# v_m times the input weights in pairs of blocks, on half rows and quarter columns of TensorE

## The chip, the cores and the metric

The kernel runs on one core of one Trainium2 chip. A core has a matrix engine (TensorE, in the profile PE, with its weight loads as PEld), which multiplies a stationary operand of up to 128 rows by 128 columns by a moving operand and writes to banks of PSUM; three elementwise engines, VectorE (DVE), ScalarE (ACT) and GpSimd (POOL); and DMA queues, here issued from SyncE (SP). Each engine works through its own instructions in order and waits on semaphores for the others. The metric is the device time of one execution in microseconds. The kernel before took 1661.22 us (median of 3 runs, 1661.06 to 1661.4).

## The reference

For 8 batches of 8 heads, 576 tokens, head size 64 and 32 memory slots, the reference compresses keys and values to 32 slots a head, attends to them, and puts the 4608 tokens through two pairs of dense layers:

```
a = softmax(phi) over the 32 slots
k_m = einsum('bhsm,bhsd->bhmd', a, k);  v_m = einsum('bhsm,bhsd->bhmd', a, v)
attn = softmax(q @ k_m.T / 8) over the slots
x = (attn @ v_m) as 4608 tokens x 512 (head h has columns 64h to 64h+63)
h = x @ w_in (512 x 2048);  g = max(0.01*h, h);  x = g @ w_out
out = (sigmoid(x @ w_gate) * (x @ w_val)) @ w2_out
```

What matters here is that `attn @ v_m @ w_in` is computed as `attn @ (v_m @ w_in)`: for each batch the product of v_m (32 slots of 8 heads, so 256 rows) and w_in is made once, and the tokens' attention is multiplied by that.

## The kernel before

**Two halves.** Until about 837 us the kernel does attention and the first pair of layers, batch by batch; after that the gated pair, which the change does not touch.

**Units and parts.** The attention of a batch is two units `(b, g)` of four heads each: unit 0 has heads 0 to 3, unit 1 heads 4 to 7. A unit is cut into parts: `t1`, `t2`, `t7a`, `t7b`, `t4`, `t5`, `t8a`, `t8b` are TensorE work, and `v1` to `v11` the work of the other engines between them. `t4` makes k_m and v_m of the four heads in one PSUM bank (`ps_kv`), 16 matmuls of 128 rows by 32 columns and 4 of 64 rows, each head on its own quarter of the columns. `v5` scales them by the softmax sums: two ACT copies (L520) write k_m and v_m with a mask, so that each head's 64 columns stand in the left or right half and zeros in the other. `t5` transposes that (`ps_kvT`), `v6` copies it to `kvT`. `t8a`, `t8b` make the scores (`ps_sc`), which `v8a`, `v8b` transpose out of PSUM on DVE (L577).

**v_m times w_in.** `vw_block(b, j)` (L646 to L660) makes 256 columns of the product, block j of 8, for both units: four matmuls (L651) of all 128 rows by 64 columns, with 256 moving columns each, into one PSUM bank `ps_vw` of 512 columns. Half of each stationary operand's entries are the zeros of the mask. The operands are plain fp32, for which the trace shows two matmul records and two weight loads to one instruction. Its `done()` evacuates the bank with `split`: an ACT copy to a rounded high part (L160) and a DVE subtraction for the low part (L161), both 128x512.

**Steps.** The first pair of layers is 256 steps, 32 a batch: a step is one half of the batch's tokens (288) by 128 of the 2048 middle columns. `m1_in` (L678) multiplies the attention (`at_hi`, `at_lo`) by 128 columns of the batch's `vw` into `ps_h`, 6 matmuls; an ACT activation reads `ps_h` (L683, `gr`); `split` makes `gh` on ACT and `gl` mostly on POOL; `m1_out` (L700) multiplies these by `w_out` into four accumulators, 12 matmuls. The main loop at step i issues: the split of step i+1; `m1_in` of step i+2; the `v` parts of units and the conversion jobs of that step, round robin (`run(vs)`), at their head the `done()` of a block from the step before (`held`); the `t` parts; a `vw_block`, if one is due; and last `m1_out` of step i. So a block's bank is read out one step after it is made.

**What sets the order.** Numbers in `SCHED`: `chain` and `chain1` give the step of each part from the unit's start, `unit` and `units` the starts, and `vw`, `vw1`, `vw2` the steps at which the 8 blocks of a batch are made (counted from the start of the batch before; `vw1` and `vw2` from the first step). Blocks of batch 0 are made by `first_vw` while weights are still being converted. The `t` parts and the blocks share two PSUM banks (`psa`, pool `ps_a`), taken in turn: each new user waits until the one two before has been read out. The `vw` tiles have nine buffers.

Of the kernel before, what the change touches and what calls it, by code (L numbers as in the profile page):

```python
# [8 lines left out]
F32 = mybir.dt.float32  # L9
# [47 lines left out]
           'v11': 16},  # L57
 'units': [1, 13, 30, 42],
 'unit': [-8, 8],
# [3 lines left out]
 'groups': [4, 4, 4, 2, 1, 1],  # L63
 'chain1': {'lp': -9,
            'lk': -4,
# [28 lines left out]
def tile_kernel(  # L94
# [42 lines left out]
    gp = ctx.enter_context(tc.tile_pool(name="g", bufs=3))  # L137
    p1 = ExitStack()
    cvp = p1.enter_context(tc.tile_pool(name="cvp", bufs=2))
    dr = ctx.enter_context(tc.tile_pool(name="dr", bufs=1, space=bass.MemoryType.DRAM))  # L140
    ps_acc = ctx.enter_context(tc.tile_pool(name="ps_acc", bufs=4, space=bass.MemoryType.PSUM))
    ps_h = ctx.enter_context(tc.tile_pool(name="ps_h", bufs=2, space=bass.MemoryType.PSUM))
# [5 lines left out]

    ident = const.tile([P, P], F32, name="ident")
    ones = const.tile([P, P], F32, name="ones")  # L150
    mask = const.tile([P, 2], F32, name="mask")

    def f32(ap):
        return ap.bitcast(F32)
# [208 lines left out]

    def unit_phi(u):
        b, g = u
        hs = slice(HG * g, HG * g + HG)
        s = un.setdefault(u, {})
        s["ph"] = ap_.tile([P, HG, CC, M], F32, tag="ph", name="ph")
        if u == FIRST2:
            m = s["m0"] = wtile("vw", [P, 2 * PC], F32, "unit_a")  # L370
            s["pht"] = m[:ST, 896:1024].rearrange("p (h m) -> p h m", h=HG)
        else:
            s["pht"] = ap_.tile([ST, HG, M], F32, tag="pht", name="pht")
        nc.sync.dma_start(
            out=s["ph"].rearrange("p h c m -> p h (c m)"),
            in_=phi[b, hs, 0:SM, :].rearrange("h (p c) m -> p h (c m)", c=CC),
        )
        nc.sync.dma_start(out=s["pht"], in_=phi[b, hs, SM:S, :].rearrange("h p m -> p h m"))

    def unit_kv(u):  # L380
        b, g = u
        hs = slice(HG * g, HG * g + HG)
        s = un[u]
        if u == FIRST2:
            m1_ = cvp.tile([P, 2 * PC], F32, tag="raw", name="unit_b", bufs=2)
            m2_ = s["m2"] = cvp.tile([P, 2 * PC], F32, tag="raw", name="unit_c", bufs=2)
            flat = (pbuf.rearrange("p c f -> p (c f)")[:, 0:1024], m1_)
            s["kv"] = [t.rearrange("p (i h c d) -> p i h c d", i=2, h=2, c=CC) for t in flat]
            s["kvt"] = m2_[:ST, 0:512].rearrange("p (i h d) -> p i h d", i=2, h=HG)
        else:  # L390
            t = ap_.tile([P, 2, HG, CC, D], F32, tag="kv", name="kv")
            s["kv"] = [t[:, :, 2 * j:2 * j + 2] for j in range(2)]
            s["kvt"] = ap_.tile([ST, 2, HG, D], F32, tag="kvt", name="kvt")
        for i, src in enumerate((k, v)):
            for j in range(2) if u == FIRST2 else (None,):
                dst = t[:, i] if j is None else s["kv"][j][:, i]
                hj = hs if j is None else slice(hs.start + 2 * j, hs.start + 2 * j + 2)
                nc.sync.dma_start(
                    out=dst.rearrange("p h c d -> p h (c d)"),
                    in_=src[b, hj, 0:SM, :].rearrange("h (p c) d -> p h (c d)", c=CC),  # L400
                )
            nc.sync.dma_start(out=s["kvt"][:, i], in_=src[b, hs, SM:S, :].rearrange("h p d -> p h d"))

    def unit_q(u):
        b, g = u
        hs = slice(HG * g, HG * g + HG)
        s = un[u]
        if u == FIRST2:
            s["q"] = obuf.rearrange("p c f -> p (c f)")[:, 0:1024].rearrange("p (c h d) -> p c h d", c=CC, h=HG)
            s["qt"] = s["m2"][:ST, 512:768].rearrange("p (h d) -> p h d", h=HG)  # L410
        else:
            s["q"] = ap_.tile([P, CC, HG, D], F32, tag="q", name="q")
            s["qt"] = ap_.tile([ST, HG, D], F32, tag="qt", name="qt")
        for c in range(CC):
            nc.sync.dma_start(
                out=s["q"][:, c], in_=q[b, hs, 0:SM, :].rearrange("h (p c) d -> c p h d", c=CC)[c],
            )
        nc.sync.dma_start(out=s["qt"], in_=q[b, hs, SM:S, :].rearrange("h p d -> p h d"))
# [4 lines left out]
    def psa(name):  # L423
        return ps_a.tile([P, 512], F32, tag="a", name=name)
# [82 lines left out]
    def v5(u):  # L507
        s = un[u]
        p = s.pop("p")
        r = ap_.tile([P, 2], F32, tag="r", name="r", bufs=2)  # L510
        nc.vector.tensor_scalar_add(r[:, 0:1], p[:, 4 * D:4 * D + 1], 1e-9)
        yield
        nc.vector.reciprocal(r[:, 0:1], r[:, 0:1])
        yield
        nc.vector.tensor_scalar_mul(r, mask, r[:, 0:1])
        yield
        x = etile(u)
        x = s["x"] = x.rearrange("p a m -> p (a m)")[:, 0:4 * D].rearrange("p (a f) -> p a f", a=2)
        for j in range(2):
            nc.scalar.activation(  # L520
                x[:, :, j * D:(j + 1) * D], p[:, 0:2 * D].rearrange("p (a d) -> p a d", a=2), AF.Copy, scale=r[:, j:j + 1]
            )
        yield

# [118 lines left out]
        for i in range(2):  # L643
            PARTS[n + "ab"[i]] = lambda u, f=f, i=i: f(u, i)

    def vw_block(b, j):  # L646
        p = psa("ps_vw")
        for g in range(NG):
            t = kvT[b, g]
            for i in range(2):  # L650
                nc.tensor.matmul(  # L651
                    p[64 * i:64 * i + 64, g * VB:(g + 1) * VB],
                    t[:, 1, 64 * i:64 * i + 64], win[j][:, 2 * g + i, :], start=True, stop=True,
                )
        def done():
            t = vw[b, j] = wtile("vw", [P, 2, NG, VB], F32R, "vw")
            split(p.rearrange("p (g f) -> p g f", g=NG), t[:, 0], t[:, 1])
            yield

        return done  # L660

    hps = {}
    gt = {}
# [286 lines left out]
    with tc.manual_schedule():  # L950
        make_identity(nc, ident)
        nc.vector.memset(ones, 1.0)
        nc.vector.memset(mask, 0.0)
        for h in range(HG):
            nc.vector.memset(mask[32 * h:32 * h + 32, h % 2:h % 2 + 1], 1.0)

# [66 lines left out]
        VW_AT = {b: [(b - 1) * NS + x for x in SCHED["vw"]] for b in range(3, B)}  # L1023
        VW_AT[0] = {i: n + NVB - len(SCHED["vw0"]) for n, i in enumerate(SCHED["vw0"])}
        VW_AT[1], VW_AT[2] = SCHED["vw1"], SCHED["vw2"]

# [8 lines left out]

        def first_vw(j):
            done_until(4 * j + 2)
            return vw_block(0, j)

        def unit_parts(i):  # L1040
            vs, ts_, ls = [], [], []
# [68 lines left out]
        for i, (b, hf, fc) in enumerate(steps):  # L1110
            if fin:
                fin()
                fin = None
            if i + LA < len(steps):
                fin = step_in(*steps[i + LA])
            else:
                if not tmps:
                    tmp_open()
                next(first)
                next(first)  # L1120
            vs, ts_, ls = unit_parts(i)
# [12 lines left out]
            run(vs)  # L1134
            for f, u in ts_:
                f(u)
            if i in VW_AT[0]:
                held = first_vw(VW_AT[0][i])
            for n in {b, b + 1} - {0}:
                if i in VW_AT.get(n, []):  # L1140
                    held = vw_block(n, VW_AT[n].index(i))
            m1_out(b, hf, fc)
            for f, u in ls:
                f(u)
            if b == B - 1:
# [69 lines left out]
```

## Time and profile before

| | before |
|---|---|
| median of 3 runs | 1661.22 us |
| the profiled execution, its whole time | 1660.55 us |
| its span, first to last instruction | 1658.8 us |
| PE busy | 1606.2 us, 97% of the span |
| DVE, ACT, POOL busy | 853.0, 681.1, 434.6 us |
| PE busy with `ps_vw` (L651) | 71.4 us, 512 records |

The page gives the busy time of each engine, a strip of the span in 40 slices, the chain of work that ended last, and the costliest groups of instructions. The profiled execution is 1.75 us longer than its span, and 0.67 us shorter than the median. Matmuls are pipelined: each record's duration holds its way through the array, so records overlap, and what a group of matmuls costs is read from start to start.

### The profile page before, as it was taken

The page shows a single profiled execution, that of the slowest core. Times are in us where ns is not written, and L with a number is a line of the kernel's source. Part 1 is how long each engine was busy: PE and PEld are TensorE (multiplying, and loading weights), DVE is VectorE, ACT ScalarE, POOL GpSimd, SP SyncE. Part 2 cuts the span into 40 slices and gives each one's busy share as a digit, 9 for nine tenths or more (in the row PEclk, how much of TensorE's full clock was granted, in tenths as well). Part 3 has the DMA queues.
Part 4 walks back from the last instruction along what each step waited for, and adds up shares of the span by engine and source line. Part 5 has one row for each costly group of instructions (what it writes and reads, how often), then busy time and mean ns, then how long its engine had stood idle before and what let it go on. Part 6 is the DMA issues. An engine that isn't in the chain of part 4 may idle for free.

```text
span 1658.8 us, 26089 instructions
## 1 busy us (share of the span) xinstructions
PE 1606.2 (97%) x9976; PEld 1390.8 (84%) x9976; DVE 853.0 (51%) x1467; ACT 681.1 (41%) x1516; POOL 434.6 (26%) x429
## 2 busy tenths in 40 slices
PE   4688999999999999999999999999999999999998
PEld 2577898989899898989988888888888888888897
DVE  6998555454454455532133655454653465354544
ACT  4664455555455555544532223331333142222332
POOL 2777343454434444443300002000200011000100
PEclk8799999999999999999999999999999999999999
DMA  9712353454445354412455466564475456546692
GB/s 297 264 45 76 105 167 102 138 158 148 135 135 168 109 156 130 148 65 78 142 154 191 139 200 192 167 219 146 144 257 176 142 170 219 167 137 201 210 401 77
DMA packets 169021, 268.58 MB, mean 162 GB/s; under 512 B 60608, under 2 KB 105664, under 8 KB 168896
## 3 DMA queue, kind: packets, MB, share of 16 engines
q1 hardware_dynamic: 168896, 266.91, 51.1%
q8 instruction: 79, 1.29, 0.3%
q14 instruction: 46, 0.38, 0.1%
HBM read 219.68 MB, written 47.19 MB: 161 GB/s over the span
## 4 chain that ended last, share of the span: by engine, by line
PE 58%; DMA 0%; DVE 0%; ACT 0%; issue 0%; SPq 0%; ACTq 0%
PE oacc L906 18%; PE ps_y L808 13%; PE ps_z L808 9%; PE ps_x L808 9%; PE acc L700 6%; PE ps_h L678 3%; PE ps_vw L651 0%; DMA gvs<-hl 0%; PE ps_kv L502 0%; PE ps_sc L567 0%; DVE hl L298 0%; PE ps_qT L550 0%; DVE st L603 0%; ACT e L596 0%; DVE osum L917 0%
## 5 line engine op out<-in xcount | busy, mean ns | idle before, releaser
L700 PE MATMUL acc<-gh,wo 128*128 128x288 f32 x2048 | 433.7, 304 | 0.6 <-ACT gh L160 0.6
L700 PEld LDWEIGHTS acc<-gh,wo 128*128 128x128 f32 x2048 | 326.3, 189 | 37.8 <-ACT gr L683 19.5
L161 POOL TENSOR_TENSOR gl<-gr,gh 128x288 fp32r<-128x288 f32 x250 | 221.5, 889 | 333.4 <-ACT gh L160 206.2
L700 PE MATMUL acc<-gl,wo 128*128 128x288 f32 x1024 | 303.7, 297 | 1.9 <-POOL gl L161 1.9
L906 PE MATMUL oacc<-w2t,pt 128*128 128x512 f32 x1296 | 296.3, 389 | 0.0
L906 PEld LDWEIGHTS oacc<-w2t,pt 128*128 128x128 f32 x1296 | 243.1, 188 | 50.3
L808 PE MATMUL ps_y<-xo,wt 128*128 128x512 f32 (+1 forms) x1080 | 251.9, 369 | 0.0
L683 ACT ACTIVATE gr<-ps_h 128x288 f32<-128x288 f32 x256 | 105.6, 413 | 325.7 <-PE ps_h L678 294.6
L678 PE MATMUL ps_h<-at_hi,vw 128*128 128x288 f32 x1024 | 213.6, 297 | 8.5 <-ACT vw L160 6.6
L808 PEld LDWEIGHTS ps_y<-xo,wt 128*128 128x128 f32 x1080 | 190.4, 188 | 33.9
L771 POOL TENSOR_TENSOR xo<-xr,xo 128x512 fp32r<-128x512 f32 (+1 forms) x16 | 23.0, 1460 | 671.0 <-ACT xo L767 671.0
L700 PEld LDWEIGHTS acc<-gl,wo 128*128 128x128 f32 x1024 | 193.3, 189 | 2.8 <-POOL gl L161 2.6
L678 PEld LDWEIGHTS ps_h<-at_hi,vw 128*128 128x128 f32 x1024 | 166.1, 190 | 9.6 <-ACT vw L160 7.5
L808 PE MATMUL ps_z<-xo,wt 128*128 128x512 f32 (+1 forms) x720 | 167.4, 368 | 0.3 <-ACT pt L843 0.3
L808 PE MATMUL ps_x<-xo,wt 128*128 128x512 f32 (+1 forms) x720 | 167.5, 368 | 0.0
L678 PE MATMUL ps_h<-at_lo,vw 128*128 128x288 f32 x512 | 151.4, 296 | 0.0
L808 PEld LDWEIGHTS ps_x<-xo,wt 128*128 128x128 f32 x720 | 127.2, 188 | 22.9
L808 PEld LDWEIGHTS ps_z<-xo,wt 128*128 128x128 f32 x720 | 127.1, 189 | 23.0 <-ACT pt L843 0.5
L843 ACT CAST pt<-sg 128x512 fp32r<-128x512 f32 (+1 forms) x120 | 69.6, 580 | 182.1 <-DVE sg L836 182.1
L161 DVE TENSOR_TENSOR vw<-ps_vw,vw 128x512 fp32r<-128x512 f32 x64 | 44.1, 691 | 183.1 <-ACT vw L160 183.1
L160 ACT CAST gh<-gr 128x288 fp32r<-128x288 f32 x256 | 112.0, 437 | 1.6
L678 PEld LDWEIGHTS ps_h<-at_lo,vw 128*128 128x128 f32 x512 | 97.1, 190 | 0.0
(155 smaller groups left out, 1804.3 us busy)
## 6 DMA issues: line engine op xcount, KB each, us to landing
wt<-gvs SPq DMA_DIRECT2D x210, 512.0 KB, 4.5
w2t<-w2s SPq DMA_DIRECT2D x60, 512.0 KB, 5.8
gvs<-hl SPq DMA_DIRECT2D x84, 256.0 KB, 2.3
x2s<-obuf SPq DMA_DIRECT2D x15, 576.0 KB, 3.5
win<-in_moe_w_in_dram SPq DMA_DIRECT2D x16, 512.0 KB, 8.9
wo_bits<-in_moe_w_out_dram SPq DMA_DIRECT2D x16, 512.0 KB, 9.0
xr<-x2s SPq DMA_DIRECT2D x16, 512.0 KB, 6.5
q<-in_q_dram SPq DMA_DIRECT2D x60, 128.0 KB, 5.1
```

The lines of the kernel that those rows point to most:

```text
L160: nc.scalar.copy(hi, raw)
L161: eng.tensor_sub(lo, raw, f32(hi))
L678: nc.tensor.matmul(p[:, :HALF], w, x, start=(n == 0), stop=(n == 3 * NG - 1))
L683: nc.scalar.activation(gr, p[:, :HALF], AF.Prelu, alpha=0.01)
L700: nc.tensor.matmul(a[d][:, :HALF], w[:, ds_], x, start=(open_ and n == 0), stop=(close and n == 2),)
L771: eng.tensor_sub(t[:, 1, :h], x_operand(n, k, a), f32(t[:, 0, :h]))
L808: nc.tensor.matmul(bank, w[:, l, a, :], x[:, r, :h], start=(start and i == 0), stop=(i == 5), skip_group_check=not start,)
L843: nc.scalar.copy(d[:, 0, :h], s)
L906: nc.tensor.matmul(bank[i], pt[2 * f + t][:, l, q * P:(q + 1) * P], w2t[f][:, r, :], start=(f == 0 and l + r == 0), stop=(f == TH - 1 and ...
```

## The change

- Unit g now has every second head (g, g+2, g+4, g+6): the four inputs are viewed as `b (h g) s d`. Shapes, sizes and number of the loads stay.
- `v5` writes k_m as before, but v_m otherwise. For batches 1 to 7 it puts each head's v_m in both halves (one ACT copy of 128x128 that reads its source twice); k_m takes two copies of 128x64. For batch 0 v_m goes into half g alone, zeros into the other, with two more mask columns; that is four copies of 128x64.
- Batch 0: `vw_block(j)` makes a block with eight matmuls of 128 rows by 32 columns instead of four of 64 columns; evacuation as before.
- Batches 1 to 7: `vw_pair(b, j0)` makes two blocks at once, with 16 matmuls of 64 rows (half g of the array, where unit g's copy lies) by 32 columns (a head's quarter). Unit g writes to its own bank; so a pair takes both banks of `ps_a`. In program order the halves alternate, then the quarters, then the block.
- The pair's evacuation is issued in the same step, behind the step's other work: four ACT copies and four DVE subtractions of 128x256. `held` is left to batch 0.
- Four pairs a batch instead of eight blocks, at other steps: 20, 22, 36, 38 (the last batch 20, 22, 25, 28; batch 1 at 26, 28, 31, 37; batch 2 at 54, 57, 59, 63).

```diff
- 'vw': [20, 21, 22, 23, 25, 27, 31, 33],
- 'vw1': [25, 27, 28, 29, 31, 33, 37, 39],
- 'vw2': [54, 55, 57, 59, 64, 68, 71, 73],
+ 'vw': [20, 22, 36, 38],
+ 'vw_last': [20, 22, 25, 28],
+ 'vw1': [26, 28, 31, 37],
+ 'vw2': [54, 57, 59, 63],
...
+    q, k, v, phi = (x.rearrange("b (h g) s d -> b g h s d", g=NG) for x in (q, k, v, phi))
...
         for j in range(2):
+            nc.scalar.activation(x[:, 0, j * D:(j + 1) * D], p[:, 0:D], AF.Copy, scale=r[:, j:j + 1])
+        if u[0] == 0:
+            for j in range(2):
+                m = 2 if j == u[1] else 3
+                nc.scalar.activation(x[:, 1, j * D:(j + 1) * D], p[:, D:2 * D], AF.Copy, scale=r[:, m:m + 1])
+        else:
             nc.scalar.activation(
-                x[:, :, j * D:(j + 1) * D], p[:, 0:2 * D].rearrange("p (a d) -> p a d", a=2), AF.Copy, scale=r[:, j:j + 1]
+                x[:, 1, :].rearrange("p (a d) -> p a d", a=2),
+                p[:, D:2 * D].rearrange("p (a d) -> p a d", a=1).to_broadcast([P, 2, D]), AF.Copy, scale=r[:, 2:3],
             )
...
+    def vw_pair(b, j0):
+        js = (j0, j0 + 1)
+        ps = [psa("ps_vw") for _ in range(NG)]
+        for n, j in enumerate(js):
+            for h in range(HG):
+                for g in range(NG):
+                    nc.tensor.matmul(
+                        ps[g][M * h:M * h + M, n * VB:(n + 1) * VB],
+                        kvT[b, g][D * g:D * g + D, 1, M * h:M * h + M],
+                        win[j][D * g:D * g + D, h, :], start=True, stop=True,
+                    )
+        for j in js:
+            vw[b, j] = wtile("vw", [P, 2, NG, VB], F32R, "vw")
+        for g in range(NG):
+            for n, j in enumerate(js):
+                split(ps[g][:, n * VB:(n + 1) * VB], vw[b, j][:, 0, g], vw[b, j][:, 1, g])
...
-                    held = vw_block(n, VW_AT[n].index(i))
+                    vw_pair(n, 2 * VW_AT[n].index(i))
```

On PE, at step 20 of batch 5 (where batch 6's first product is made), the program has before, from `m1_in` to the next block:

```order
L678 MATMUL ps_h<-at_hi,vw 128x288 x2
L678 MATMUL ps_h<-at_lo,vw 128x288
L651 MATMUL ps_vw<-win,kvT 64x256 x4
L700 MATMUL acc<-gh,wo 128x288 x2
L700 MATMUL acc<-gl,wo 128x288
```

and now, at the same step:

```order
L705 MATMUL ps_h<-at_hi,vw 128x288 x2
L705 MATMUL ps_h<-at_lo,vw 128x288
L678 MATMUL ps_vw<-win,kvT 32x256 x16
L727 MATMUL acc<-gh,wo 128x288 x2
L727 MATMUL acc<-gl,wo 128x288
```

The product stands at the same place between `m1_in` of step i+2 and `m1_out` of step i; four instructions became sixteen of half the output rows, and the block that stood in the next step is gone.

On ACT, at step 37 (part `v5` of batch 2's first unit, `e<-ps_kv,r`), before:

```order
L160 CAST gh<-gr 128x288
L683 ACTIVATE gr<-ps_h 128x288
L520 ACTIVATE e<-ps_kv,r 128x2x64 x2
L160 CAST gh<-gr 128x288
L683 ACTIVATE gr<-ps_h 128x288
L160 CAST vw<-ps_vw 128x512
L160 CAST gh<-gr 128x288
```

and now:

```order
L162 CAST gh<-gr 128x288
L710 ACTIVATE gr<-ps_h 128x288
L521 ACTIVATE e<-ps_kv,r 128x64 x2
L527 ACTIVATE e<-ps_kv,r 128x128
L162 CAST vw<-ps_vw 128x256 x4
L162 CAST gh<-gr 128x288
L710 ACTIVATE gr<-ps_h 128x288
```

The block's copy stood behind the next step's `gh` and `gr`; the pair's four copies stand in the pair's own step, ahead of the next step's `gh`, and directly behind the copies out of `ps_kv`, whose bank the pair takes.

## Rows read from the trace of the kernel before

**Rows 1.** The page: busy time (share of the span) and instructions.

```profile
PE 1606.2 (97%) x9976; PEld 1390.8 (84%) x9976; DVE 853.0 (51%) x1467; ACT 681.1 (41%) x1516; POOL 434.6 (26%) x429
```

**Rows 2.** Busy time by stretch, all engines; columns as in the first line.

```profile
core 0: us, PE busy (x) PEld busy (x) DVE busy (x) ACT busy (x) POOL busy (x), PEclk, DMA share, GB/s
...
560.00:660.00 100.00, 100.00 (x797) 90.42 (x796) 48.63 (x97) 53.20 (x138) 43.72 (x46) 1.00 0.47 136
```

**Rows 3.** Who waited for whom on PE, 160 to 840 us: total, times, longest.

```profile
PE acc L700 <- POOL gl L161: 0.4, 1, 0.4
PE acc L700 <- ACT gh L160: 0.2, 1, 0.2
```

**Rows 4.** Groups by line and shape: busy us, mean ns of one.

```profile
L651 PE MATMUL ps_vw<-win,kvT 128*64 128x256 f32 x512 | 71.4, 400 | 5.9 <-POOL win L210 4.1 <-issue 1.7
...
L541 ACT COPY kvT<-ps_kvT 128x256 f32<-128x256 f32 x16 | 5.9, 369 | 1.2 <-PE ps_kvT L531 1.2
...
L879 DVE TENSOR_TENSOR sg<-ps_y,tmp 128x256 f32<-128x256 f32 x6 | 2.5, 425 | 6.5 <-PE ps_y L808 6.5
```

**Rows 5.** PE in order of time, a step with a block, 664 to 669 us.

```profile
664.83 0.43 PE L678 MATMUL ps_h<-at_hi,vw 128*128 128x288 f32 x2
...
665.49 0.29 PE L678 MATMUL ps_h<-at_lo,vw 128*128 128x288 f32 x1
665.71 1.08 PE L651 MATMUL ps_vw<-win,kvT 128*64 128x256 f32 x8
666.73 0.53 PE L700 MATMUL acc<-gh,wo 128*128 128x288 f32 x2
667.10 0.29 PE L700 MATMUL acc<-gl,wo 128*128 128x288 f32 x1
...
668.42 0.43 PE L678 MATMUL ps_h<-at_hi,vw 128*128 128x288 f32 x2
```

**Rows 6.** The same, a step without block or unit part.

```profile
776.90 0.42 PE L678 MATMUL ps_h<-at_hi,vw 128*128 128x288 f32 x2
...
779.30 0.43 PE L678 MATMUL ps_h<-at_hi,vw 128*128 128x288 f32 x2
```

**Rows 7.** The first records of the block alone (narrow window).

```profile
665.71 0.44 PE L651 MATMUL ps_vw<-win,kvT 128*64 128x256 f32 x2
```

**Rows 8.** `t4`: quarter columns, at 661 and at 23 us.

```profile
661.53 1.08 PE L502 MATMUL ps_kv<-kv,e 128*32 128x128 f32 x32
662.54 0.42 PE L502 MATMUL ps_kv<-kvt,pht 64*32 64x128 f32 x8
...
23.46 0.43 PE L502 MATMUL ps_kv<-pbuf,unit_a 128*32 128x128 f32 x2
23.48 0.43 PE L502 MATMUL ps_kv<-unit_b,unit_a 128*32 128x128 f32 x2
```

**Rows 9.** Step 37: the block and the copies out of `ps_kv`.

```profile
195.61 1.08 PE L651 MATMUL ps_vw<-win,kvT 128*64 128x256 f32 x8
...
196.09 0.62 ACT L520 ACTIVATE e<-ps_kv,r 128x128 f32<-128x128 f32 x2
```

**Rows 10.** Step 63: the end of `m1_in` and the copies out of `ps_kv`.

```profile
275.59 0.30 PE L678 MATMUL ps_h<-at_lo,vw 128*128 128x288 f32 x1
...
276.59 0.63 ACT L520 ACTIVATE e<-ps_kv,r 128x128 f32<-128x128 f32 x2
```

**Rows 11.** Steps 19 and 20 of batch 5: scores, their transpose, the block.

```profile
625.94 0.71 PE L567 MATMUL ps_sc<-qT,kvT 128*64 128x288 f32 x4
...
626.70 0.48 DVE L577 STREAM_TRANSPOSE e<-ps_sc 128x288 f32<-128x288 f32 x1 [0.25 <-PE ps_sc L567]
...
629.14 1.08 PE L651 MATMUL ps_vw<-win,kvT 128*64 128x256 f32 x8
```

**Rows 12.** PE's waits for the copies of `v5`, whole span.

```profile
PE ps_kvT L529 <- ACT e L520: 2.7, 1, 2.7
...
PE ps_kvT L529 <- ACT unit_a L520: 2.3, 1, 2.3
```

More of the change, by code (lines that the diff above doesn't have):

```diff
@@ L150, in tile_kernel @@
     ones = const.tile([P, P], F32, name="ones")
-    mask = const.tile([P, 2], F32, name="mask")
+    mask = const.tile([P, 4], F32, name="mask")
     def f32(ap):
@@ L365, in unit_phi @@
         b, g = u
-        hs = slice(HG * g, HG * g + HG)
         s = un.setdefault(u, {})
@@ L375, in unit_phi @@
             out=s["ph"].rearrange("p h c m -> p h (c m)"),
-            in_=phi[b, hs, 0:SM, :].rearrange("h (p c) m -> p h (c m)", c=CC),
+            in_=phi[b, g, :, 0:SM, :].rearrange("h (p c) m -> p h (c m)", c=CC),
         )
-        nc.sync.dma_start(out=s["pht"], in_=phi[b, hs, SM:S, :].rearrange("h p m -> p h m"))
+        nc.sync.dma_start(out=s["pht"], in_=phi[b, g, :, SM:S, :].rearrange("h p m -> p h m"))
     def unit_kv(u):
         b, g = u
-        hs = slice(HG * g, HG * g + HG)
         s = un[u]
@@ L396, in unit_kv @@
                 dst = t[:, i] if j is None else s["kv"][j][:, i]
-                hj = hs if j is None else slice(hs.start + 2 * j, hs.start + 2 * j + 2)
+                hj = slice(0, HG) if j is None else slice(2 * j, 2 * j + 2)
                 nc.sync.dma_start(
                     out=dst.rearrange("p h c d -> p h (c d)"),
-                    in_=src[b, hj, 0:SM, :].rearrange("h (p c) d -> p h (c d)", c=CC),
+                    in_=src[b, g, hj, 0:SM, :].rearrange("h (p c) d -> p h (c d)", c=CC),
                 )
-            nc.sync.dma_start(out=s["kvt"][:, i], in_=src[b, hs, SM:S, :].rearrange("h p d -> p h d"))
+            nc.sync.dma_start(out=s["kvt"][:, i], in_=src[b, g, :, SM:S, :].rearrange("h p d -> p h d"))
     def unit_q(u):
         b, g = u
-        hs = slice(HG * g, HG * g + HG)
         s = un[u]
@@ L415, in unit_q @@
             nc.sync.dma_start(
-                out=s["q"][:, c], in_=q[b, hs, 0:SM, :].rearrange("h (p c) d -> c p h d", c=CC)[c],
+                out=s["q"][:, c], in_=q[b, g, :, 0:SM, :].rearrange("h (p c) d -> c p h d", c=CC)[c],
             )
-        nc.sync.dma_start(out=s["qt"], in_=q[b, hs, SM:S, :].rearrange("h p d -> p h d"))
+        nc.sync.dma_start(out=s["qt"], in_=q[b, g, :, SM:S, :].rearrange("h p d -> p h d"))
     def unit_engine(part, u):
@@ L509, in v5 @@
         p = s.pop("p")
-        r = ap_.tile([P, 2], F32, tag="r", name="r", bufs=2)
+        r = ap_.tile([P, 4], F32, tag="r", name="r", bufs=2)
         nc.vector.tensor_scalar_add(r[:, 0:1], p[:, 4 * D:4 * D + 1], 1e-9)
@@ L644, in tile_kernel, with vw_block @@
             PARTS[n + "ab"[i]] = lambda u, f=f, i=i: f(u, i)
-    def vw_block(b, j):
+    def vw_block(j):
         p = psa("ps_vw")
         for g in range(NG):
-            t = kvT[b, g]
-            for i in range(2):
+            for h in range(HG):
                 nc.tensor.matmul(
-                    p[64 * i:64 * i + 64, g * VB:(g + 1) * VB],
-                    t[:, 1, 64 * i:64 * i + 64], win[j][:, 2 * g + i, :], start=True, stop=True,
+                    p[M * h:M * h + M, g * VB:(g + 1) * VB],
+                    kvT[0, g][:, 1, M * h:M * h + M], win[j][:, h, :], start=True, stop=True,
                 )
         def done():
-            t = vw[b, j] = wtile("vw", [P, 2, NG, VB], F32R, "vw")
+            t = vw[0, j] = wtile("vw", [P, 2, NG, VB], F32R, "vw")
             split(p.rearrange("p (g f) -> p g f", g=NG), t[:, 0], t[:, 1])
@@ L660, in vw_block @@
         return done
+    def vw_pair(b, j0):
+        js = (j0, j0 + 1)
+        ps = [psa("ps_vw") for _ in range(NG)]
+        for n, j in enumerate(js):
+            for h in range(HG):
+                for g in range(NG):
[9 more added lines that the diff above has]
+                split(ps[g][:, n * VB:(n + 1) * VB], vw[b, j][:, 0, g], vw[b, j][:, 1, g])
     hps = {}
@@ L953, in tile_kernel @@
         nc.vector.memset(mask, 0.0)
+        nc.vector.memset(mask[:, 2:3], 1.0)
         for h in range(HG):
@@ L1023, in tile_kernel @@
         VW_AT = {b: [(b - 1) * NS + x for x in SCHED["vw"]] for b in range(3, B)}
+        VW_AT[B - 1] = [(B - 2) * NS + x for x in SCHED["vw_last"]]
         VW_AT[0] = {i: n + NVB - len(SCHED["vw0"]) for n, i in enumerate(SCHED["vw0"])}
@@ L1037, in first_vw @@
             done_until(4 * j + 2)
-            return vw_block(0, j)
+            return vw_block(j)
         def unit_parts(i):
```

## The prediction

> **What bounds the kernel now.** I read the busy times first: PE is busy 97% of the span, no other engine much over half [rows 1]. Busy PE alone proves little, because pipelined records overlap. So I looked at the stretches and the waits: from 160 us on, PE has work in every slice of the half that the change touches, while DVE, ACT and POOL stand at 44 to 53 of 100 us [rows 2]; and from 160 to 840 us PE waited three times in all, 0.6 us together [rows 3]. So in that half time is what PE's instructions take from start to start, and an instruction stream that takes PE less time shortens the kernel by as much, until a new wait appears. Seven of the eight batches' products, 56 of 64 blocks, are made there or just before (batch 1's first at about 157 us). Batch 0's lie in the opening stretch, where PE waits for other engines.
>
> **What a block costs.** Between two starts of `m1_in`, a step with a block takes 668.42 - 664.83 = 3.59 us [rows 5], one without block or unit part 779.30 - 776.90 = 2.40 us [rows 6]. A block costs PE 1.19 us: from the last record of `m1_in` to the first of the block 0.22 us, 1.02 us until `m1_out` starts, and a slower start of `m1_out`, less what these gaps are without a block. Inside it are eight records: four instructions, each two records. They run two at a time: in a window that ends at 665.96 two records have begun and no third [rows 7], on the two column halves. Hence four rounds. The block lasts 1.08 us from first start to last end and one record 0.40 us [rows 4, 5], so a round takes (1.08 - 0.40)/3 = 0.22 to 0.23 us; I use 0.22.
>
> **What a pair costs.** It has 16 instructions, so 32 records, each again of 256 columns. The question is how many run at once. The nearest row is `t4`: quarter columns, all rows [rows 8]. There 32 records of 128 columns take 1.01 us from start to start of the next group. Taken alone at half of 0.22 they would need 3.5 us, so four run at once. The opening stretch, where the operands have different names, shows it directly: four records start within 0.02 us at 23.46 and 23.48. The same row settles the issue rate: 32 records and their loads pass through PE's queue in 1.01 us, as many as a pair has. That both halves of the rows also run side by side, so eight at once, no row of this trace shows. The bounds are: eight at once, four rounds, the time of a block, 1.19 us; four at once, eight rounds, 1.19 + 4 x 0.22 = 2.07 us; one at a time, 1.19 + 28 x 0.22 = 7.35 us. Nothing excludes values between; less than four rounds is excluded, as each tile has four records to stream. I take eight at once, because the nearest row shows that tiles on separate columns cost nothing beside each other, the two halves read different rows of the operands and write different banks, and the program alternates them; with 0.04 us for four more staggered starts a pair is 1.23 us.
>
> The Trainium skill states this case: TensorE: Matmul & The Clock Gate, section Part 3: Packing small matmuls, says that row and column tiles compose, up to sixteen at once, started some 4 ns apart. By it a pair would be the four rounds above. No run here shows it yet.
>
> **Gain.** Two blocks cost 2.38 us, a pair 1.23 us: 1.15 us saved, times 28 pairs = 32.2 us. Between four and eight at once it is 28 x (2.38 - 2.07) = 8.7 us to 28 x (2.38 - 1.19) = 33.3 us.
>
> **Batch 0's blocks** become eight instructions on quarter columns: sixteen records, by fours as in `t4`, four rounds as before. Nothing, either way.
>
> **Waits that the change adds.** A pair takes both banks of `ps_a`, so PE also waits for the bank used last; behind it stand `m1_out` of the same step and everything after. Most pairs follow `t8b` by one step. Its bank is read by a DVE transpose, which ends at 626.70 + 0.48 = 627.18 us, while the block in the next step starts at 629.14 us [rows 11]: 2 us of cover, cost nothing. Two pairs, at steps 37 and 63, stand one step behind `t4` instead, whose bank `v5` reads on ACT behind that step's `gr`. At step 37 these copies end at 196.09 + 0.62 = 196.71 us, and `v5` now has a third, 0.31 us by the two in that row, while the pair would start at 195.61 [rows 9]: PE waits 1.4 us. At step 63 the copies would end at 276.59 + 0.63 + 0.31 = 277.53 us, and the pair could start 0.22 us behind 275.59 [rows 10]: 1.7 us. Together 3.1 us; zero if ACT happens to run ahead, twice that if conversion copies slip in between.
>
> **The evacuation.** Four ACT copies at 0.37 us, each followed on DVE by a subtraction at 0.43 us [rows 4]: both banks are free about 1.9 us behind the pair, the first sooner. What wants a bank next comes one step later at the earliest, behind `m1_out` (1.6 us) and `m1_in` (0.8 us), two thirds and one third of 2.40 [rows 6]; 0.5 us of cover in the tightest case. On ACT the next step's `gh` is queued behind the four copies, and POOL's `gl` behind that: some 2.8 us behind the pair, wanted two steps later, 4.8 us behind it. The `vw` tiles are wanted two steps later at the earliest as well. ACT's 112 copies are 41 us over some 600 us in which it idles half the time [rows 2], and they replace 56 longer ones. Cost nothing; if the cover went, a wait of a few tenths at each of 28 pairs.
>
> **`v5` and the loads.** One more copy a unit (two more in batch 0), 0.31 us each. In batches 1 to 7 `t5` stands two steps behind `t4`: hidden, except at the two pairs above. In batch 0, PE waited 2.7 and 2.3 us for these copies [rows 12], so up to 2 x 0.62 = 1.2 us may show, or none, since weight conversion on DVE is waited for later; I take 0.6 us. The loads keep their number, sizes and place in SP's queue; only strides change: nothing.
>
> **Sum.** -32.2 + 3.1 + 0.6 = -28.5 us. From the profiled execution's 1660.55 us that gives 1632.0 us; the median lies 0.67 us higher, so 1632.7 us.
>
> **Rivals.**
>
> *The halves take turns.* The two row halves of a quarter share the columns below them; if they can't both deliver, a pair needs eight rounds, 2.07 us. This is also the case in which the change doesn't do what it says. Gain 8.7 us, less 3.7 us: 1656.2 us. For it: no row shows half rows side by side. Against: separate banks, and the quarters in `t4` show no sharing.
>
> *The alternation blocks (slower).* PE issues in order, and the halves alternate innermost. If a half must wait until the other has drained, the next quarter's record waits behind it, and the quarters don't overlap either: up to 7.35 us a pair, 28 x (7.35 - 2.38) = 139 us more, 1804 us with the waits. It decides as soon as a pair costs over 2.38 - 3.7/28 = 2.25 us, which is under four tiles at a time. Against it: in `t4` records of different tiles overtake no one and still start within 0.02 us [rows 8]. It needs a conflict that the columns don't have.
>
> *The evacuation binds.* Everything happens in a burst: two banks at once, four copies and four subtractions behind `gr`, and at step 20 and 36 behind the attention's exponentials. If PE waits 0.5 us at every pair, for a bank or a `vw` tile, 14 us are lost: 1646.7 us. For it: only 0.5 us of cover where a `t` part follows at once (five pairs of batches 1 and 2). Against: 2 us or more elsewhere. The Trainium skill warns of this: TensorEngine Tiling (Array Packing), section Performance Considerations, says that tiling speeds up the matmuls but not the reading of PSUM, which may become the limit. The trace agrees with the fixed cost behind it: reading a pair takes some 1.9 us against 1.2 us of matmuls. It decides here only if steps in between were as short as the pairs, and they are not.
>
> **How the numbers follow.** Forecast 0.74, with its own range from 1627 us (no new wait shows, the pair at 1.19 us) to 1641 us (the two waits doubled, 1.2 us in the opening, and 0.2 us at each pair); evacuation 0.08, turns 0.10, blocking 0.06; 0.02 for no change by gains lost in several places. The range must reach the turns to leave out less than 2 in 10: 1627 to 1657 us. A measurement here can tell 0.2%, 3.3 us, from no change. Faster: 0.74 + 0.08 + 0.09 of the turns = 0.91. Same: 0.03. Slower: 0.06.
>
> **What would show it.** In the profile after: `ps_vw` records of 64 rows by 32 columns, 32 in some 1.1 us from first start to last end (right), or about 2 us (turns), or more (blocking); busy PE with `ps_vw` falling from 71.4 to some 40 us; the next `m1_out` 1.0 us behind a pair's start. PE's waits from 160 us on should name ACT's copies of `v5` twice, 1 to 2 us each, and little else; waits for `vw` or for DVE at many pairs mean the evacuation. `m1_in` to `m1_in` should be 3.6 us over a step with a pair. I am wrong if half rows don't run side by side; everything else moves the time by single microseconds.

## The result, and the profile after

The changed kernel took 1639.5 us (median of four runs, 1638.95 to 1641.8) against 1661.2 us: a ratio of 0.987, with a 95% interval of 0.986 to 0.988. It is 1.3% faster, and the time lies inside the predicted range, 6.8 us above the predicted 1632.7 us. The profiled execution took 1639.72 us, its span is 1637.9 us, 20.9 us shorter than that of the kernel before.

PE is still the bound. The page of the changed kernel, busy time; below it the stretch of [rows 2] (columns as there):

```profile
PE 1579.2 (96%) x10488; PEld 1378.0 (84%) x10488; DVE 857.4 (52%) x1524; ACT 691.0 (42%) x1590; POOL 439.1 (27%) x429
```
```profile
560.00:660.00 100.00, 100.00 (x892) 92.32 (x891) 49.54 (x105) 56.49 (x154) 47.20 (x50) 1.00 0.51 155
```

**The pair.** Groups by line and shape (busy us, mean ns of one, idle time before), then one pair in order of time, and the same pair in a window of 0.05 us:

```profile
L163 DVE TENSOR_TENSOR vw<-ps_vw,vw 128x256 fp32r<-128x256 f32 x112 | 44.8, 421 | 76.0 <-ACT vw L162 76.0
L162 ACT CAST vw<-ps_vw 128x256 fp32r<-128x256 f32 x112 | 38.8, 373 | 44.9 <-DVE vw L163 36.1 <-PE ps_vw L678 8.7
L678 PE MATMUL ps_vw<-win,kvT 64*32 64x256 f32 x896 | 32.5, 382 | 2.5 <-ACT e L527 1.7 <-DVE mx L449 0.8
L659 PE MATMUL ps_vw<-win,kvT 128*32 128x256 f32 x128 | 12.1, 463 | 5.7 <-POOL win L212 4.0 <-issue 1.7
```
```profile
663.75 0.43 PE L705 MATMUL ps_h<-at_hi,vw 128*128 128x288 f32 x2
...
664.42 0.29 PE L705 MATMUL ps_h<-at_lo,vw 128*128 128x288 f32 x1
664.64 1.09 PE L678 MATMUL ps_vw<-win,kvT 64*32 64x256 f32 x32
...
665.66 0.54 PE L727 MATMUL acc<-gh,wo 128*128 128x288 f32 x2
...
667.36 0.42 PE L705 MATMUL ps_h<-at_hi,vw 128*128 128x288 f32 x2
```
```profile
664.64 0.45 PE L678 MATMUL ps_vw<-win,kvT 64*32 64x256 f32 x8
```

In 0.05 us eight records have begun and no ninth. The pair's 32 records take 1.09 us, where eight records of a block took 1.08 [rows 5], and the step takes 667.36 - 663.75 = 3.61 us, as a step with a block did. `m1_out` follows 1.02 us behind the pair's start. Busy PE with `ps_vw` is 32.5 + 12.1 = 44.6 us, against 71.4 [rows 4]. So a pair takes four rounds, the fewest that it can.

**The waits.** Who waited for whom on PE from 160 to 840 us (total, times, longest), where there was 0.6 us in all before [rows 3]:

```profile
PE acc L727 <- DVE obuf L734: 1.7, 1, 1.7
PE ps_vw L678 <- ACT e L527: 1.7, 2, 1.0
PE acc L727 <- POOL gl L163: 1.6, 5, 0.4
PE acc L727 <- DVE pbuf L734: 1.0, 1, 1.0
PE ps_vw L678 <- DVE mx L449: 0.8, 1, 0.8
```

Only the second line was predicted. A line gives idle time alone; what a wait costs, with the records that it slows, I read from the starts of `m1_in` in the steps around it: 1.3 us at step 37, 1.6 at 63, 1.4 at 57 (`mx`), 1.95 at 29 (`obuf`), 1.2 at 32 (`pbuf`), and 0.5 to 0.75 us at five steps (88, 90, 104, 152, 200) behind four pairs of batches 3 to 6, 3.0 us together (`gl`).

**The evacuation** of the pair of 167.85 us (step 28), ACT and DVE in order of time, and what PE waited for behind it:

```profile
169.89 0.37 ACT L162 CAST vw<-ps_vw 128x256 fp32r<-128x256 f32 x1
...
170.29 0.42 DVE L163 TENSOR_TENSOR vw<-ps_vw,vw 128x256 fp32r<-128x256 f32 x1 [1.11 <-ACT vw L162]
...
170.75 0.65 ACT L162 CAST vw<-ps_vw 128x256 fp32r<-128x256 f32 x2 [0.49 <-DVE vw L163]
171.15 0.76 DVE L163 TENSOR_TENSOR vw<-ps_vw,vw 128x256 fp32r<-128x256 f32 x2 [0.44 <-ACT vw L162]
171.94 0.37 ACT L162 CAST vw<-ps_vw 128x256 fp32r<-128x256 f32 x1 [0.55 <-DVE vw L163]
172.34 0.42 DVE L163 TENSOR_TENSOR vw<-ps_vw,vw 128x256 fp32r<-128x256 f32 x1 [0.44 <-ACT vw L162]
172.68 1.54 DVE L734 TENSOR_TENSOR obuf<-acc,obuf 128x288 f32<-128x288 f32 x4
...
173.28 0.51 PE L727 MATMUL acc<-gh,wo 128*128 128x288 f32 x2 [1.72 <-DVE obuf L734]
```

ACT's second copy waits for DVE's subtraction, though it reads other columns: it is the second half of the same bank. So copies and subtractions take turns, and the burst lasts 172.76 - 169.89 = 2.87 us, not 1.9. It does so in 21 of the 28 pairs; in the other seven DVE's first subtraction comes late as well, and the burst lasts 3.2 to 5.0 us. Behind it on DVE stand the four adds (L734) that close an accumulator of batch 0, and `m1_out` of the next step needs those banks.

### The profile page after: what moved, and what is told of

Read it like the earlier page. It is cut to its first block, busy times and chain, and to the rows that moved or that the text cites. A ratio compares the mean times of both kernels' runs of the same rounds, so it can differ in the third digit from the quotient of the medians.

```text
span 1637.9 us, 27232 instructions
## 1 busy us (share of the span) xinstructions
PE 1579.2 (96%) x10488; PEld 1378.0 (84%) x10488; DVE 857.4 (52%) x1524; ACT 691.0 (42%) x1590; POOL 439.1 (27%) x429
## 4 chain that ended last, share of the span: by engine, by line
PE 75%; DMA 1%; ACT 1%; DVE 1%; issue 1%; POOL 0%; SPq 0%; ACTq 0%; POOLq 0%; DVEq 0%
PE oacc L933 18%; PE acc L727 16%; PE ps_y L835 13%; PE ps_x L835 9%; PE ps_z L835 9%; PE ps_h L705 7%; PE ps_vw L678 1%; DMA wt<-gvs 1%; PE ps_kv L503 1%; PE ps_sc L575 1%; PE ps_qT L558 0%; DVE vw L163 0%; DMA gvs<-hl 0%; ACT vw L162 0%; POOL gl L163 0%
## 5 line engine op out<-in xcount | busy, mean ns | idle before, releaser
L163 POOL TENSOR_TENSOR gl<-gr,gh 128x288 fp32r<-128x288 f32 x250 | 225.0, 904 | 353.6 <-ACT gh L162 263.7
L944 DVE TENSOR_TENSOR osum<-oacc,osum 128x512 f32<-128x512 f32 x72 | 49.6, 689 | 81.5 <-PE oacc L933 81.4
```

The lines of the kernel that those rows point to most:

```text
L944: nc.vector.tensor_add(o, bank[i], o)
```

## The experiments

The kernel before, beside the runs below, took 1660.5 to 1661.7 us. Single waits are smaller than the spread of the times, so each run's trace is also compared step by step. The table gives, against the first trace of the kernel before, how far the 26th `m1_in` starts later or earlier (the opening), and by how much the stretch from there to the last `m1_in` is shorter (28 pairs lie in it).

| run | time, us | 26th `m1_in` | from there to the last |
|---|---|---|---|
| changed kernel, first profile | 1639.5 | +2.8 | -23.8 |
| after_again | 1640.1 | +4.1 | -23.8 |
| evac_alternating | 1634.7 | +3.1 | -29.4 |
| vw1_moved | 1638.3 | +3.8 | -25.5 |
| vw2_moved | 1637.6 | +1.3 | -25.4 |
| halves_in_turn (one run) | 1643.9 | +3.8 | -20.7 |
| quarter_by_quarter (one run) | 1640.5 | +1.9 | -22.7 |
| same_rows (one run) | 1660.2 | +2.3 | -2.8 |
| batch0_as_before | 1641.3 | +1.2 | -22.2 |
| combined | 1630.6 | +1.3 | -32.0 |
| combined_batch0 | 1634.8 | +0.3 | -32.3 |
| before_again, before_third (one run each) | 1662.0, 1661.0 | +1.7, +0.8 | +0.1, -0.3 |

### The measure

> The changed kernel once more, as the measure for the runs beside it. Expected 1639.5 us, ratio 0.986 to 0.988, with the same waits in the same steps: 1.3 us ahead of the pair at step 37, 1.6 at 63, 1.4 at 57, and 1.9 and 1.2 us ahead of m1_out at steps 29 and 32. If the slow start of m1_in at steps 22 and 23 comes from the change and not from a chance dip of the granted clock, it is here again.

1640.1 us (1638.1 to 1645.0; ratio 0.986 to 0.990). The waits stand at the same steps with the same sizes. The opening was another 1.3 us longer. Parts of it ran at a granted clock of 0.5 (1.2 GHz) again: from 147.1 us on, near the place of the first profile (146.5 us), and here from 130.1 us on too.

### The order of the evacuation

```diff
-        for g in range(NG):
-            for n, j in enumerate(js):
+        for n, j in enumerate(js):
+            for g in range(NG):
                 split(ps[g][:, n * VB:(n + 1) * VB], vw[b, j][:, 0, g], vw[b, j][:, 1, g])
```

> Only the order of the evacuation is changed: the second ACT copy reads the other unit's bank instead of the other half of the same bank. Theory: in the changed kernel ACT's second copy out of a bank waits for the DVE subtraction that reads the same bank, so four copies and four subtractions take 2.9 us one after the other; with alternating banks they overlap, 4 x 0.37 + 0.43 = 1.9 us from the first copy to the end of the last subtraction. The two waits of m1_out for the closing adds of batch 0 (steps 29 and 32) then shrink by about 0.9 us each, nothing else moves: 1637.7 us. Rival: the copies and subtractions are slow because two engines read PSUM at once, whatever the bank; then the chain stays at 2.9 us and the time at 1639.5 us.

1634.7 us (1633.4 to 1635.7; ratio 0.983 to 0.986, apart from the measure's). One burst in order of time, and PE's waits from 160 to 840 us:

```profile
667.82 0.64 ACT L162 CAST vw<-ps_vw 128x256 fp32r<-128x256 f32 x2
668.22 1.62 DVE L163 TENSOR_TENSOR vw<-ps_vw,vw 128x256 fp32r<-128x256 f32 x4 [0.27 <-ACT vw L162]
668.67 0.70 ACT L162 CAST vw<-ps_vw 128x256 fp32r<-128x256 f32 x2 [0.22 <-DVE vw L163]
```
```profile
PE ps_vw L678 <- ACT e L527: 1.7, 2, 1.0
PE ps_vw L678 <- DVE pht L475: 0.4, 1, 0.4
```

The burst is 669.84 - 667.82 = 2.0 us, in 24 of the 28 pairs; single copies and subtractions are as long as before. So the alternation inside a bank was the cause, not two readers of PSUM as such. The gain is 5.6 us by the table, three times what I expected: beside 1.7 us at step 29 and 0.9 at step 32, the five waits for `gl` are gone as well (3.0 us). There ACT, held up in the burst, had come late to the next step's `gh`, and POOL late to `gl`.

### Where batch 1's pairs stand

```diff
- 'vw1': [26, 28, 31, 37],
+ 'vw1': [26, 33, 37, 39],
```

> Only batch 1's pairs are moved, from steps 26, 28, 31, 37 to 26, 33, 37, 39, away from the steps that close batch 0's accumulators. Theory: at steps 28 and 31 the adds that close the accumulators stand on DVE behind the pair's four subtractions and m1_out of the next step waits for them; with the pairs moved these two waits go (1.95 + 1.24 = 3.2 us less), and the new places cost between nothing and the 1.3 us that step 37 costs already, one of them behind t5, whose bank ACT reads: about 1637 us. Rival: m1_out waits for these adds because adds of four banks behind m1_out take longer than one m1_in, with or without a pair; then steps 29 and 32 keep their waits and the time stays at 1639.5 us or rises by the new places.

1638.3 us (ratio 0.985 to 0.988), which by itself is not apart from the measure. By steps: the waits at 29 and 32 are gone (-1.95 and -1.24 us), steps 33 and 37 cost 0.2 us more each, and at 39 a new wait of 1.2 us appears, for the copy that reads the bank of `t5` (`qT`). PE's waits from 160 to 840 us:

```profile
PE ps_vw L678 <- ACT e L527: 1.9, 2, 1.0
PE acc L727 <- POOL gl L163: 1.5, 5, 0.4
PE ps_vw L678 <- DVE mx L449: 0.6, 1, 0.6
PE ps_vw L678 <- DVE qT L551: 0.6, 1, 0.6
```

So the adds wait because of the pair ahead of them on DVE, not by themselves: the theory.

### Where batch 2's pairs stand

```diff
- 'vw2': [54, 57, 59, 63],
+ 'vw2': [54, 59, 68, 70],
```

> Only batch 2's pairs are moved, from steps 54, 57, 59, 63 to 54, 59, 68, 70: 68 stands behind t8b and 70 behind no part. Theory: the wait at 63 is the wait for v5's copies out of the bank that the pair takes (1.6 us), the one at 57 the wait for v2, which is late on DVE (1.4 us); both are of the place, so both go and the new places cost nothing: 3.0 us less, 1636.5 us. Rival: the waits belong to the burst of four copies and four subtractions that comes with each pair, and reappear at 68 and 70: 1639.5 us.

1637.6 us (ratio 0.985 to 0.988). The wait at 63 went, all 1.6 us, and steps 68 and 70 cost a bare pair (1.2 us). Of the wait at 57 most came back two steps on: PE waits 0.4 us for `dg` (L452), and the pair at 59 is slowed to 1.50 us by `pht` (L475). By the starts these two cost 0.6 and 0.4 us. Both belong to the same chain on DVE. So 63 was a matter of the place, 57 only in part: there DVE is late with the next unit, pair or no pair. DVE in the changed kernel around the pair at 57 (PE, `ps_vw`), in order of time:

```profile
256.61 0.78 DVE L633 STREAM_TRANSPOSE atr<-e 128x576 f32<-128x576 f32 x1 [1.27 <-POOL e L617]
257.31 0.38 DVE L195 TENSOR_SCALAR y<-y 128x512 f32<-128x512 f32 x1
257.44 0.62 PE L678 MATMUL ps_vw<-win,kvT 64*32 64x256 f32 x2
257.73 0.90 DVE L198 TENSOR_SCALAR y<-y 128x512 int32<-128x512 int32 x1
258.55 0.28 DVE L449 TENSOR_REDUCE mx<-ps_t 128x1 f32<-128x128 f32 x1
...
258.88 0.88 PE L678 MATMUL ps_vw<-win,kvT 64*32 64x256 f32 x23 [0.82 <-DVE mx L449]
```

### What makes eight at once

```diff
-        for n, j in enumerate(js):
-            for h in range(HG):
-                for g in range(NG):
+        for g in range(NG):
+            for n, j in enumerate(js):
+                for h in range(HG):
```

> Only the program order of the pair's sixteen instructions is changed: all eight of unit 0 (rows 0 to 63) first, then all eight of unit 1, the four quarters alternating. The same 32 records, the same tiles. Theory: a pair costs 1.22 us because both row halves stream at once, eight tiles; with the halves in turn only four tiles stream at once, except where the halves meet, so eight rounds of 0.22: 2.1 us a pair, 28 x 0.87 = 24 us more, 1664 us. Rival: what runs at once is picked by PE from a queue, whatever the program order; then the pair stays at 1.22 us and the time at 1640 us.

1643.9 us: the theory, that program order decides what runs at once, is refuted. One pair, in windows of 0.03 and 0.15 us and whole:

```profile
622.33 0.42 PE L678 MATMUL ps_vw<-win,kvT 64*32 64x256 f32 x4
```
```profile
622.33 0.47 PE L678 MATMUL ps_vw<-win,kvT 64*32 64x256 f32 x8
```
```profile
622.33 1.12 PE L678 MATMUL ps_vw<-win,kvT 64*32 64x256 f32 x32
```

Four records of unit 0 begin; 0.05 us later (0.13 in other pairs) four of unit 1 run beside them, although in the order of the compiled program twelve more records of unit 0 stand ahead of them. The pair takes 1.12 us. Four of the 28 pairs, at steps 37, 57, 59 and 63, do run one half behind the other: there unit 1's bank came free late, and its records start 1.0 to 2.7 us behind unit 0's. At step 59, where the changed kernel does not wait, the 32 records thus take 2.10 us, as long as the theory gave a pair. Of the 3.1 us that the stretch is longer, 1.3 us come at step 37 and 0.95 us at step 59; the other pairs take some hundredths more each (0.06 us on the mean), and the waits for `gl` are 0.5 us shorter.

```diff
-        for n, j in enumerate(js):
-            for h in range(HG):
+        for h in range(HG):
+            for n, j in enumerate(js):
                 for g in range(NG):
```

> Again only the order of the sixteen instructions: quarter by quarter, in each quarter unit 0, unit 1 of the first block, then unit 0, unit 1 of the second. A record finds its tile busy after every second instruction. Theory: PE starts records in order, so a record that waits for its own tile holds back those of free tiles behind it; at most the two halves of one quarter stream at once, and the last round of a quarter lies beside the first of the next: 4 x 4 - 3 = 13 rounds of 0.22 instead of 4, 1.22 + 9 x 0.22 = 3.2 us a pair, 28 x 2.0 = 56 us more, 1695 us. This is the mechanism of the rival that the alternation blocks, with its price in this kernel. Rival: free tiles are served past a waiting one, 1.22 us a pair, 1640 us.

1640.5 us; refuted again. The pair of 664.64 us:

```profile
664.64 1.13 PE L678 MATMUL ps_vw<-win,kvT 64*32 64x256 f32 x32
665.70 0.54 PE L727 MATMUL acc<-gh,wo 128*128 128x288 f32 x2
```

1.13 us, not 3.2: PE serves a free tile past records that wait for theirs. 0.04 us a pair is 1.1 us in 28, the table's difference. A record that waits for its bank is another matter: in the changed kernel's pair at step 37 (198.02 us) unit 0's first two records start, and the other thirty, of both units, stand until 1.3 us later, when unit 1's bank is free.

```diff
-                        kvT[b, g][D * g:D * g + D, 1, M * h:M * h + M],
-                        win[j][D * g:D * g + D, h, :], start=True, stop=True,
+                        kvT[b, g][0:D, 1, M * h:M * h + M],
+                        win[j][0:D, h, :], start=True, stop=True,
```

> Both units' products of a pair use rows 0 to 63 of TensorE; unit 1 thereby multiplies with the weights of unit 0's heads, so its part of the product is another than the reference's. The 32 records, their sizes, the two banks and everything else stay as in the changed kernel; only the second row half is not used, and each of four tiles has eight records to stream. Theory: a pair costs 1.22 us because the two row halves stream side by side; without them eight rounds of 0.215: 1.22 + 4 x 0.215 = 2.1 us, 28 x 0.86 = 24 us more, 1664 us. This is the price of the rival that the halves take turns. Rival: the rows have nothing to do with it, and what allows eight at once is the two banks or the sixteen separate instructions: 1.22 us a pair, 1640 us.

1660.2 us: the theory holds. One pair, and `m1_out` behind it:

```profile
680.36 1.97 PE L678 MATMUL ps_vw<-win,kvT 64*32 64x256 f32 x32
682.26 0.40 PE L727 MATMUL acc<-gh,wo 128*128 128x288 f32 x1
```

Same records, same banks, one row half: `m1_out` follows 1.90 us behind the start instead of 1.02, so 0.88 us more a pair, 24.6 us in 28. The stretch grew by 21.0 us; the rest is waits that the slower PE no longer has (the `gl` waits are gone, the adds wait 1.4 us instead of 2.7), less 1.5 us that step 63 costs more. So the row halves side by side are what makes this change worth 21 us instead of 1.5 (1660.2 beside 1661.7 us).

### The opening

```diff
+    def heads(x, b, g):
+        return x[b, HG * g:HG * g + HG] if b == 0 else x[b].rearrange("(h g) s d -> g h s d", g=NG)[g]
...
+        if u[0] == 0:
+            for j in range(2):
+                nc.scalar.activation(
+                    x[:, :, j * D:(j + 1) * D], p[:, 0:2 * D].rearrange("p (a d) -> p a d", a=2), AF.Copy, scale=r[:, j:j + 1]
+                )
...
-                    p[M * h:M * h + M, g * VB:(g + 1) * VB],
-                    kvT[0, g][:, 1, M * h:M * h + M], win[j][:, h, :], start=True, stop=True,
+                    p[64 * i:64 * i + 64, g * VB:(g + 1) * VB],
+                    kvT[0, g][:, 1, 64 * i:64 * i + 64], win[j][:, 2 * g + i, :], start=True, stop=True,
```

> Batch 0 is done as in the kernel before: heads 0 to 3 and 4 to 7 in its units, v5 with two ACT copies instead of four, blocks of four instructions of 64 columns. Everything from batch 1 on is as changed. Theory: the two more copies of v5 in batch 0 start m1_in later by 0.2 to 0.9 us, so this run begins m1_in 0.6 us sooner and ends at 1639 us. Rival: the opening stretch, which differs by 1 us and more between runs of the same kernel, costs more because of the change (2.8 us at step 24 in the first profile, of it 1.7 us at half clock); then this kernel is 2 to 3 us faster, 1637 us, and the dip of the granted clock at 147 us is gone.

1641.3 us (1639.6 to 1643.3), no gain in time. The edit takes back loads, `v5` and blocks of batch 0 together, so by itself it names none of them. The opening is 1.2 us behind instead of 2.8 or 4.1. The stretch behind it is 1.6 us longer, by 0.5 to 0.7 us each at steps 71, 104 and 200; PE's waits for `gl` there are 2.5 us instead of 1.6. Why they grow with the older batch 0 stays open.

> The kernel before once more, for a second trace of its opening stretch. The eight traces so far whose first 158 us run the same instructions as the changed kernel lie 1.3 to 4.1 us behind the first trace of the kernel before at the 26th m1_in, 0.2 to 0.9 us at the first. Theory: the first 0.2 to 0.9 us are the change's (v5's two more copies in batch 0), the rest is spread between runs, which the kernel before has too: this trace lies within 0.2 us of the first one at the first m1_in and 0 to 3 us behind it at the 26th. Rival: the opening belongs to the change as a whole; then this trace lies within 0.3 us of the first one at both places.

> As the run ahead of it, a third trace of the opening stretch of the kernel before: by the theory 0 to 3 us behind the first at the 26th m1_in, by the rival within 0.3 us.

The kernel before (no edit) spreads too, by 0, 1.7 and 0.8 us at the 26th `m1_in`, by 0, 0.4 and 0.7 at the first. The changed openings lie at 0.2 to 0.9 (mean 0.6) at the first, 1.3 to 4.1 (mean 2.7) at the 26th. So `v5`'s copies are not told from the spread at the first `m1_in`, while on the mean some 2 us are lost up to the 26th that the kernel before and the two runs with its batch 0 (1.2 and 0.3) don't lose.

The steps show a part of these 2 us. Counted from its own first `m1_in` and against the first trace of the kernel before, the ninth `m1_in` is 0.55 to 0.60 us late in all nine changed traces, and at most 0.03 us late in the five with the older batch 0. Of this, 0.27 us is batch 0's fourth block, which takes 1.34 us in all nine and 1.08 us in all five. The second block takes some 5.5 us instead of some 4.7, but it stands ahead of the first `m1_in`, and no run shows whether that waits for it. Most of the rest follows the granted clock: in four of the nine traces it falls to 0.5 at 145 to 147 us, and these lose 1.5 to 2.9 us between the 21st and the 26th `m1_in`; the other five lose 0.3. Before it fell, PE had waited 1.8 to 2.9 us for `v5`'s copies (L527). In the combined run PE waited 2.9 us there too, and the clock stayed at 1.0. In the five traces with the older batch 0 it does not fall there; whether that is the change or chance stays open.

### Together

The edit of the evacuation, and:

```diff
- 'vw1': [26, 28, 31, 37],
- 'vw2': [54, 57, 59, 63],
+ 'vw1': [26, 28, 31, 33],
+ 'vw2': [54, 55, 68, 70],
```

> Three edits at once: the alternating evacuation; batch 1's pairs at 26, 28, 31, 33 (the last one away from v5's copies at 37); batch 2's at 54, 55, 68, 70 (away from v2 at 57 and 59 and from v5 at 63). Theory: on top of the alternating evacuation's 1634.7 us the waits at 37 (1.3 us), 57 and 59 (1.6 us together in that run) and 63 (1.6 us) go, 0.2 us comes at 33: 1630.4 us, and from 160 us on PE waits less than 1 us in all. Rival: the two pairs in a row at 54 and 55 keep ACT and DVE late, and a wait of 1 to 2 us appears there: 1632 us.

1630.6 us (1630.3 to 1631.3; ratio 0.980 to 0.983): faster than both kernels. PE's waits from 160 to 840 us:

```profile
PE ps_vw L678 <- DVE pht L475: 0.6, 1, 0.6
PE ps_vw L678 <- DVE vw L163: 0.3, 1, 0.3
```

The first line is the pair at 33, which waits for `pht`'s read of `t2`'s bank on DVE: by the starts 1.2 us, where I had expected 0.2. The second line is the pair at 55, which waits for the burst of the pair at 54; the rival named the place, but it costs 0.7 us by the starts, not 1 to 2.

That 1630.6 us is what I expected (1630.4) is in part luck: against the alternating evacuation alone the stretch gained 2.6 us by the table instead of 4.3, and the opening of the profiled run happened to be 1.8 us shorter.

The last run adds to it the edit of the opening.

> The three edits of the combined run, and batch 0 done as in the kernel before. At the 26th m1_in the nine traces with the changed batch 0 lie 1.3 to 4.1 us behind the first trace of the kernel before (mean 2.7), three traces of the kernel before 0 to 1.7 (mean 0.8), the run with batch 0 as before 1.2. Theory: batch 0's new form costs the opening 1 to 2 us, and giving it back makes 1629 us out of 1630.6. Rival: the opening is spread between runs only, and the 1.6 us that the run with batch 0 as before lost behind the opening come with that form; then 1631 to 1632 us.

1634.8 us (1629.8 to 1635.9), not faster. The profiled run shows both halves of the story: the opening and the pairs gave 1.3 us more than in the combined run (+0.3 and -32.3 in the table), and then, at the start of the gated pair, PE waited for a weight transfer:

```profile
PE ps_z L838 <- DMA wt<-gvs: 2.5, 1, 2.5
```

In batch0_as_before the same wait is 1.4 us, in the changed kernel 0.2 us. Why that transfer is later with the older batch 0 stays open. The profiled run took 1631.9 us, 2.8 us less than the median of the five, so this wait does not account for the median.

## Why the prediction was right, and where it was off

Right was the main term. A pair in its step costs 1.22 us (predicted 1.23), a block 1.20, so a pair saves 2 x 1.20 - 1.22 = 1.18 us, and 28 of them 33.0 us (predicted 32.2). The choice between eight and four at once was made by the row nearest to it [rows 8], and same_rows shows what it was worth: 21 us. Right by size were the two waits behind `v5`, 1.3 and 1.6 us (predicted 1.4 and 1.7 from [rows 9, 10]).

Off was the rest of the sum, -28.5 us against a measured -20.9 us:

- **The evacuation** was put at 1.9 us and at nothing. It took 2.9 us. The step that failed is the one from four copies, each followed by a subtraction, to both banks free about 1.9 us behind the pair: it took ACT and DVE for a pipeline, and looked at the lengths but not at whether the second copy may start while DVE reads the same bank. The cover that I had counted for ACT's next `gh` (2.8 us behind the pair, wanted at 4.8) was then short behind four of the 28 pairs, at five steps: 3.0 us. That is the rival of the evacuation that binds, behind four pairs instead of all. The Trainium skill has the rule that I passed over: PSUM — Partial Sum Buffer, section PSUM bank collisions raise a hardware error, says that two engines may not read the same bank on the same partitions at once, even in different columns, and that the compiler's scheduler therefore makes instructions on different engines which touch one bank depend on each other. The trace agrees: ACT's copies wait 0.49 and 0.55 us for DVE's reads. By it the burst is the chain copy, subtraction and copy in turn, as measured.
- **The queue behind the subtractions.** I named what stands behind the four copies on ACT, but not what stands behind the four subtractions on DVE. At steps 28 and 31 that is an add that PE waits for in the next step: 1.95 + 1.24 = 3.2 us, of which the alternating order alone gave back 2.6.
- **Step 57** was counted among the pairs with 2 us of cover. It follows `t1`, whose bank `v2` reads on DVE, and DVE was behind: 1.4 us. I had checked two places one by one and taken the others by the pattern.
- **The opening** was put at 0.6 us for `v5`, and batch 0's blocks at nothing. The first `m1_in` is 0.6 us late on the mean, which the spread of the kernel before covers; up to the 26th it was 2.8 us in this profile. Batch 0's fourth block alone costs 0.27 us, and some 1.4 us of the 2.8 came with the half clock at 146.5 us.

Added up: -33.0 + 2.9 + 3.2 + 1.4 + 3.0 + 2.8 = -19.7 us. The remaining -1.2 us is a wait of the kernel before that the prediction left out. It read 0.6 us in three waits from [rows 3], which show two; both lie in step 200 (691.16 us), which takes 694.81 - 691.16 = 3.65 us there, where like steps take 2.50. The changed kernel's own wait at that step is among the 3.0 us for `gl`.

All four terms above made the gain smaller. The time still lies in the range because the main term carries it. It is near the upper end of the forecast's own range, 1641 us, which allowed 0.2 us at each pair without saying where; that the losses at single steps came to no more is luck.

The rivals: *turns* has its price in same_rows and does not happen. *Blocking* is excluded by quarter_by_quarter, for a reason that I had not given: a record that waits for its tile does not hold back those of other tiles. The rule of the Trainium skill named in the prediction (TensorE: Matmul & The Clock Gate, Part 3: Packing small matmuls), that row and column tiles compose, agrees with the trace: eight records begin within 0.05 us, some 7 ns apart. The same section of the Trainium skill says that matmuls start and end in program order; halves_in_turn differs, as unit 1's records start ahead of unit 0's later ones, and the measurement decides.

## What to carry to other kernels

Where a change makes one engine's work come in a burst, list for each engine of the burst what is queued behind it, not only for the one whose time is cut. When two engines read one PSUM bank in turn, let consecutive reads go to different banks: here swapping two loops was worth 5 us. And a place that costs nothing by the pattern should be read once in the trace before it is counted as free.

## What the runs showed of the hardware

- TensorE starts a record on a free tile although records ahead of it in program order still wait for theirs: three orders of the same sixteen instructions take 1.09, 1.12 and 1.13 us where both banks are free. An instruction that waits for its bank does hold back those behind it: thirty records for 1.3 us in the pair at 198.02 us. Eight tiles of 64 rows by 32 columns stream at once; the eight records of a round begin within 0.05 us, rounds follow each 0.22 us.
- ACT's copy out of one half of a PSUM bank waited for DVE's read of the other half (0.49 and 0.55 us where DVE was free). It is a wait on a semaphore in the compiled program; no run here leaves it out.
- The same 150 us of program took up to 2.8 us more or less between runs, partly by stretches at a granted clock of 0.5 at changing places, while the some 660 us behind them repeat to a few tenths.
